# Retention attention and a GELU layer on one core: when each batch's loads are issued, and where batch 3's first scores stand

## The chip, the cores and the metric

The kernel runs on one core of one Trainium2 chip. Its time is the device time of one execution in microseconds (us). Before the change three runs took 295.61, 297.89 and 301.87 us, so the median is 297.89 us. A fourth execution was recorded by the hardware profiler; it took 295.5 us, and all views of the profile below are of that one.

## The reference, cut to what matters

```python
def _attn_ref(q, k, v):                       # (8, 8, 576, 64) each: batch, head, position, head width
    scores = scale * np.matmul(q, k.transpose(0, 1, 3, 2))
    gamma = 1.0 - 2.0 ** (-5.0 - np.arange(H))
    rel = pos[:, None] - pos[None, :]
    Dmat = np.where(rel >= 0, gamma[:, None, None] ** rel[None, :, :], 0.0)
    return np.matmul(scores * Dmat[None], v)

def _moe_ref(x, w_in, w_out):                 # x: 4608 x 512, w_in: 512 x 2048, w_out: 2048 x 512
    h = x @ w_in
    g = 0.5 * h * (1.0 + np.tanh(c * (h + 0.044715 * h * h * h)))
    return g @ w_out
```

The attention result of all 8 batches, with its heads side by side, is the x of the second function. Inputs and output are float32.

## The kernel before, in words

**Tiling.** A batch has 576 positions: four chunks of 128 and a tail of 64. The tails of two batches make one tile, called the tails of that pair. The second part works on blocks of 512 tokens: block t (0 to 7) is the four chunks of batch t, block 8 is made of the tails. The two parts overlap: while TensorE works through block t of the layers, it also computes, in between, the attention of batch t + 1, whose result is the x of the next block. The attention is causal with a decay, so each chunk needs its own scores (`score`, line 379), a mask (`masks`, line 389), the product with v (`av`, line 455), and what the chunks in front leave behind: a state (`state`, 402), carried on by `scan` (416) and `spread` (430) and multiplied with q in `past` (436). `put` (466) copies the finished chunk into `xT`, the input of the next block.

**Order written out by hand.** A block is a list of about 30 steps (lines 979 to 1041). In blocks 2 to 5, which matter here, steps 0 to 15 are `up` (474): four matmuls of 128x512 and a GELU on ScalarE for each. Steps 16 to 29 are `prod` (648), eight matmuls of 128x256 each, seven products computed in two halves. After every second pair of `up` steps (steps 3, 7, 11 and 15) `act_sums` (634) puts four additions on VectorE. Everything else is hung on a step by `at(t, u, f)`: after step u of block t, f is issued. The program fixes the order in which each engine gets its instructions; each engine then works through its own in that order, and waits where an input is not there.

**Attention in a block.** Lines 940 to 953 hang the attention of batch b = t + 1 into block t. `scores` (911) of chunks 0 and 1 stand after step s0, their `outs` (922: past, av, the next state, put) after step o0, the scores of chunks 2 and 3 after s1, their outs after o1. Normally (s0, o0, s1, o1) is (9, 15, 19, 25); in block 3 it is (11, 15, 19, 25). The tails of a pair go with the scores and outs of blocks 3, 4, 6 and 7 (`TP`, line 132). The scans follow one step after the outs (`later`, line 778).

**Loads, casts and transposes.** For a batch b from 2 on, 12 loads (q, k and v of four chunks, 256 KB each, `load`, line 91) go from SyncE's queue, SP, into one of 16 buffers. Each is cast to float16 by `cc` (771), k and q on GpSimd (POOL), v on ScalarE (for batch 3 on GpSimd too). The casts of batch b stand in block b - 2, from step 16 to 23 (line 958). Then `turn_dma` (305) issues two DMA transposes from SP, one for k and one for q, and, where tails go with the batch, `cast_tails` (245) casts their k and q on GpSimd and issues one more transpose, of the tile e into the tile ett. The scores of batch b in block b - 1 read what these transposes write (`tt`, `ett`).

**The queue of loads.** `seq` (line 130) lists all loads in order: the first batches and weights, then batch after batch, with an entry "t" for the loads of a pair's tails behind the batch b for which b - 1 is in `TP`. `pump` (141) issues entries from the list as long as one of the 16 buffers is free; `cc` gives a buffer back and calls it. An entry "h" makes it stop until `resume` (312), which each batch b hangs after step 29 of block b - 2 (batch 2: step 12 of block 1). Before the change "h" stands behind batches 2 and 3; from batch 4 on the queue is stopped by a line of its own from step 16, where the casts begin, to step 29. Since 16 buffers stand against 12 loads of a batch, the resume in block 1 issues the 12 loads of batch 4, the 6 of the first tails and the first 4 of batch 5; the resumes of blocks 2, 3 and 4 then issue the other 8 of a batch, its tails if any, and the first 4 of the batch after it (block 4's has none after it).

Lines that the prediction's steps touch, as they stand before:

```python
    for b in range(1, B):
        seq += body(b) if b > 1 else []
        if b in (NPE, NPE + 1):
            seq.append(("h",))
        if b - 1 in TP:
            seq.append(("t", TP[b - 1]))
...
        at(t0, 5 if b == NPE else ut[-1] + 1, lambda b=b: turn_dma(b, TP.get(b - 1)))
        at(t0, go, resume)
```

Of the kernel before, what the change touches and what calls it, by code (L numbers as in the profile page):

```python
# [20 lines left out]
def kernel(  # L21
# [22 lines left out]
    NPE = 2  # L44
# [74 lines left out]
    def parts(b):  # L119
        if b == NPE:  # L120
            return [(key, c) for c in range(NC) for key in "kq"] + [("v", c) for c in range(NC)]
        return [(key, c) for c in range(NC) for key in "kqv"]

    def body(b):
        if b < NPE:
            return [("b", b, key, 2 * g + y) for g in range(2) for key in "qkv" for y in range(2)]
        return [("b", b, *x) for x in parts(b)]

    QS = (0, 2, 1, 3)
    seq = body(0) + [("i", g, ct) for g in QS for ct in range(4)]  # L130
    seq += [("o", f) for f in range(NF)] + body(1)
    TP = {3: 0, 4: 2, 6: 4, 7: 6}
    for b in range(1, B):
        seq += body(b) if b > 1 else []
        if b in (NPE, NPE + 1):
            seq.append(("h",))
        if b - 1 in TP:
            seq.append(("t", TP[b - 1]))
    q_ld = {"next": 0, "free": LD, "hold": False}

    def pump(freed=0):
# [98 lines left out]
    def new_casts(b):  # L240
        a = att[b]
        for key in "kqv":
            a[key] = sb.tile([128, W], F16, tag="c" + key, name="c" + key, bufs=1 if key == "q" else 2)
# [38 lines left out]
    def new_turned(b):  # L282
        att[b]["tt"] = t = sb.tile([128, 2, NB, 128], F16, tag="tt", name="tt", bufs=2)
        att[b]["tk"], att[b]["tq"] = t[:, 0], t[:, 1]
# [20 lines left out]
    def turn_dma(b, tails=None):  # L305
        a = att[b]
        for key in "kq":
            nc.sync.dma_start_transpose(out=a["t" + key], in_=a[key])
        if tails is not None:
            cast_tails(tails)  # L310
# [460 lines left out]
    def cc(b, key, c, eng):  # L771
        cast(b, key, c, eng)
        pump(1)
# [4 lines left out]
    def later(b, c):  # L778
        scan(b, c)
        spread(b, c, A.copy)  # L780
# [53 lines left out]
    def at(t, u, f, last=False):  # L834
        events.setdefault((t, u, last), []).append(f)
# [75 lines left out]
    def scores(t, c, tails=None):  # L911
        b = t + 1
        if b < B:
            score(b, c), score(b, c + 1)
        if tails is not None:
            score(PAIR + tails, 0)
        if b < B:
            masks(b, c), masks(b, c + 1)
        if tails is not None:
            masks(PAIR + tails, 0)  # L920

    def outs(t, c, tails=None, ahead=None):
        b = t + 1
        work = [(b, c), (b, c + 1)] if b < B else []
        if tails is not None:
            work.append((PAIR + tails, 0))
        for w in work:
            past(*w)
        for w in work:
            av(*w)  # L930
        if ahead is not None:
            state(*ahead)
        for w in work:
            put(*w)

    U2 = (21, 23, 25, 28)
# [2 lines left out]
        at(1, 17 + c, lambda c=c: later(2, c))  # L939
    for t in range(1, B):  # L940
        b, tl = t + 1, TP.get(t)
        s0, o0, s1, o1 = U2 if t == 1 else (11, 15, 19, 25) if t == 3 else (9, 15, 19, 25)
        at(t, s0, lambda t=t, tl=tl: scores(t, 0, tl))
        at(t, o0, lambda t=t, b=b, tl=tl: outs(t, 0, tl, (b, 2, 3) if t < B - 1 else None))
        if b == B:
            continue
        at(t, s1, lambda t=t, b=b: scores(t, 2))
        at(t, o0 + 1, lambda b=b: later(b, 2))
        at(t, o1, lambda t=t, nb=b + 1: outs(t, 2, None, (nb, 0, 1) if nb < B else None))
        at(t, min(o1 + 1, 29), lambda b=b: later(b, 3))  # L950
        if b + 1 < B:
            for c in range(2):
                at(t + 1, c, lambda c=c, nb=b + 1: later(nb, c))

    for b in range(NPE, B):
        ent = parts(b)
        eng = {"k": P, "q": P, "v": P if b == NPE + 1 else A}
        t0, ut, go = b - 2, [16, 16, 17, 18, 18, 19, 20, 20, 21, 22, 22, 23], 29
        if b == NPE + 1:
            ut = [16, 16, 17, 19, 19, 20, 22, 22, 23, 24, 24, 25]  # L960
        if b == NPE:
            t0, ut, go = 1, [0, 0, 0, 0, 2, 2, 4, 4, 6, 7, 9, 10], 12
        at(t0, ut[0], lambda b=b: (new_casts(b), new_turned(b)))
        if b > NPE + 1:
            at(t0, ut[0], lambda: q_ld.update(hold=True))
        if b > NPE:
            at(t0, ut[0], lambda t=t0: nc.gpsimd.tensor_copy(out=gate, in_=gs[t]["4"][:, NH - 1, 1, 0:1]))  # L967
        for u, (key, c) in zip(ut, ent):
            at(t0, u, lambda b=b, key=key, c=c, e=eng[key]: cc(b, key, c, e))
        at(t0, 5 if b == NPE else ut[-1] + 1, lambda b=b: turn_dma(b, TP.get(b - 1)))  # L970
        at(t0, go, resume)
# [101 lines left out]
```

## Time and profile before

| what | value |
|---|---|
| time of the profiled execution | 295.5 us |
| its span, first to last instruction | 293.7 us |
| TensorE (PE) busy | 281.8 us, 96% |
| VectorE (DVE) busy | 201.0 us, 68% |
| ScalarE (ACT) busy | 169.5 us, 58% |
| GpSimd (POOL) busy | 99.9 us, 34% |
| granted TensorE clock | 0.995 of full |
| DMA, mean over the span | 184 GB/s |

The span and the time differ by 1.8 us that lie around the instructions. Busy time of an engine is the time in which it worked on an instruction; PE's weight loads are counted apart. "SP" is the engine that issues the DMAs; an entry of its queue in the timeline begins when it starts to issue a DMA and is as long as the issuing takes, while the data land some microseconds later. A wait is put down to what came last. Block 2 of the layers runs from 84.6 to 114.5 us, block 3 to 146.2, block 4 to 176.8, block 5 to 206.7.

### The profile page before, as it was taken

The page shows a single profiled execution, that of the slowest core. Times are in us where ns is not written, and L with a number is a line of the kernel's source. Part 1 is how long each engine was busy: PE and PEld are TensorE (multiplying, and loading weights), DVE is VectorE, ACT ScalarE, POOL GpSimd, SP SyncE. Part 2 cuts the span into 40 slices and gives each one's busy share as a digit, 9 for nine tenths or more (in the row PEclk, how much of TensorE's full clock was granted, in tenths as well). Part 3 has the DMA queues.
Part 4 walks back from the last instruction along what each step waited for, and adds up shares of the span by engine and source line. Part 5 has one row for each costly group of instructions (what it writes and reads, how often), then busy time and mean ns, then how long its engine had stood idle before and what let it go on. Part 6 is the DMA issues. An engine that isn't in the chain of part 4 may idle for free. (4 is left out here: it accounts for less than half of the span.)

```text
span 293.7 us, 7393 instructions
## 1 busy us (share of the span) xinstructions
PE 281.8 (96%) x3028; PEld 208.1 (71%) x3028; DVE 201.0 (68%) x409; ACT 169.5 (58%) x320; POOL 99.9 (34%) x129
## 2 busy tenths in 40 slices
PE   6989998999999999989999999999999999999993
PEld 3568876888864687458845884488548887887782
DVE  6796988656864873487448744765488968975863
ACT  5287754996338546855486647664665268507800
POOL 4689669901760184008500740068030000000000
PEclk9999999999999999999999999999999999999998
DMA  7999999999989999999999999995941030002013
GB/s 209 311 366 378 364 286 244 248 241 191 222 131 260 229 211 190 202 267 209 194 209 252 223 208 235 222 137 90 242 100 38 2 143 3 0 38 107 3 36 107
DMA packets 139361, 53.95 MB, mean 184 GB/s; under 512 B 118080, under 2 KB 130880, under 8 KB 139328
## 3 DMA queue, kind: packets, MB, share of 16 engines
q1 hardware_dynamic: 138848, 52.97, 80.8%
q8 instruction: 23, 0.38, 0.6%
q10 hardware_dynamic: 480, 0.52, 0.6%
q14 instruction: 10, 0.08, 0.1%
HBM read 36.70 MB, written 9.44 MB: 157 GB/s over the span
## 5 line engine op out<-in xcount | busy, mean ns | idle before, releaser
L480 PE MATMUL hp<-xT,w_in_sb 128*128 128x512 f16 x352 | 79.0, 380 | 0.0
L486 ACT ACTIVATE gT<-hp 128x512 f16<-128x512 f32 x88 | 50.1, 600 | 26.5 <-PE hp L480 26.0
L665 PEld LDWEIGHTS <-gT 128*128 128x128 f16 x576 | 54.9, 98 | 9.1 <-issue 1.3
L480 PEld LDWEIGHTS <-w_in_sb 128*128 128x128 f16 x352 | 34.1, 98 | 38.1
L665 PEld LDWEIGHTS <-s 128*128 128x128 f16 x432 | 41.7, 98 | 5.3
L642 DVE TENSOR_TENSOR s<-gT 128x512 f16<-128x512 f16 x36 | 15.6, 434 | 31.8 <-ACT gT L486 25.1
L665 PE MATMUL opA<-w_out_sb,gT 128*128 128x256 f16 x288 | 35.3, 273 | 0.7 <-ACT w_out_sb L765 0.6
L392 DVE TENSOR_TENSOR ret<-st,cm 128x512 f16<-128x512 f32 x48 | 29.7, 682 | 3.8 <-PE st L383 3.8
L501 PE MATMUL hp<-xT,w_in_sb 128*128 128x256 f16 x256 | 29.2, 273 | 0.3 <-POOL w_in_sb L765 0.3
L967 POOL COPY gate<-s 128x1 f16<-128x1 f16 x5 | 0.9, 188 | 82.6 <-DVE s L646 82.6
L434 ACT CAST tbd<-ws 64x256 f16<-64x256 f32 x48 | 19.3, 403 | 13.8 <-DVE ws L425 13.2
L501 PEld LDWEIGHTS <-w_in_sb 128*128 128x128 f16 x256 | 24.5, 98 | 3.6 <-POOL w_in_sb L765 0.6
L665 PE MATMUL opB<-wt,gT 128*128 128x256 f16 x224 | 26.8, 273 | 0.1
L275 POOL TENSOR_TENSOR ck<-ld,sc 128x512 f16<-128x512 f32 x24 | 25.0, 1040 | 4.4 <-DMA ld<-in_k_dram 4.4
L275 POOL TENSOR_TENSOR cq<-ld,sc 128x512 f16<-128x512 f32 x24 | 25.9, 1078 | 0.6 <-DMA ld<-in_q_dram 0.3
L469 ACT CAST xT<-xs 128x512 f16<-128x512 f32 x36 | 19.3, 592 | 11.7 <-PE xs L459 8.5
L679 DVE TENSOR_TENSOR k<-k,opB 128x512 f32<-128x512 f32 x17 | 11.7, 686 | 13.3 <-PE opB L665 7.4
L508 ACT ACTIVATE gT<-hp 128x512 f16<-128x512 f32 x32 | 18.4, 602 | 3.6 <-PE hp L501 3.5
L262 ACT CAST cv<-ld 128x512 f16<-128x512 f32 x23 | 13.4, 618 | 11.9 <-DMA ld<-in_v_dram 11.7
L665 PE MATMUL opB<-wt,s 128*128 128x256 f16 x144 | 17.4, 273 | 0.0
L665 PE MATMUL opC<-wt,s 128*128 128x256 f16 x144 | 17.2, 273 | 0.0
L644 DVE TENSOR_TENSOR gT<-gT 128x512 f16<-128x512 f16 x36 | 17.1, 476 | 0.0
(122 smaller groups left out, 407.1 us busy)
## 6 DMA issues: line engine op xcount, KB each, us to landing
ld<-in_q_dram SPq DMA_DIRECT2D x32, 256.0 KB, 5.2
ld<-in_k_dram SPq DMA_DIRECT2D x32, 256.0 KB, 5.2
ld<-in_v_dram SPq DMA_DIRECT2D x32, 256.0 KB, 5.4
out_dram<-ost SPq DMA_DIRECT2D x16, 512.0 KB, 3.9
ld<-in_moe_w_in_dram SPq DMA_DIRECT2D x16, 256.0 KB, 5.7
ld<-in_moe_w_out_dram SPq DMA_DIRECT2D x16, 256.0 KB, 6.0
lt<-in_k_dram SPq DMA_DIRECT2D x8, 128.0 KB, 4.6
lt<-in_q_dram SPq DMA_DIRECT2D x8, 128.0 KB, 4.4
```

The lines of the kernel that those rows point to most:

```text
L262: eng.copy(out=dst, in_=raw)
L275: eng.tensor_tensor(out=dst.rearrange("p (h d) -> p h d", d=D), in0=raw.rearrange("p (h d) -> p h d", d=D), in1=sc[:, s0].unsqueeze(2).to_ ...
L392: nc.vector.tensor_tensor(out=r.rearrange("p (n i) -> p n i", i=128), in0=t.rearrange("p (n i) -> p n i", i=128), in1=(cm if b < PAIR else ...
L434: cp(out=(tbd[b % 2][r, c, :, r] if c < NC - 1 else tbt[b % NT4][r, :, r]), in_=w[r])
L469: nc.scalar.copy(out=xT[:, g0 : g0 + 2], in_=xs.rearrange("p (n g t) -> p g n t", n=HP, g=2))
L480: nc.tensor.matmul(hp.rearrange("p (g t) -> p g t", t=TL), w_in_sb[:, ct, 128 * fc : 128 * fc + 128], xT[:, o : o + TB // TL, ct, :], star ...
L486: nc.scalar.activation(out=gT[t][:, fc].rearrange("p i n -> p (i n)"), in_=hp, func=AF.Gelu_apprx_tanh)
L501: nc.tensor.matmul(hps[n][:, 256 * x : 256 * x + 256].rearrange("p (g t) -> p g t", t=TL), w_in_sb[:, ct, 128 * (fs[n] + x) : 128 * (fs[n] ...
L508: nc.scalar.activation(out=gT[t][:, f : f + 2, 2 * u : 2 * u + 2, :].rearrange("p f i n -> p f (i n)"), in_=hp.rearrange("p (f n) -> p f n ...
L642: nc.vector.tensor_tensor(out=s["1"], in0=a21, in1=a22, op=ALU.add)
L644: nc.vector.tensor_tensor(out=a21, in0=a11, in1=a21, op=ALU.subtract)
L665: nc.tensor.matmul(op[tag][:, HD * u : HD * u + HD], lhs(f), rhs[:, f], start=(new and f == 0), stop=(f == NH - 1), skip_group_check=True,)
```

## The change

Two things. In the list of loads, an "h" now stands behind every batch from 2 to 7 (behind its tails, where it has some), and the old stop from step 16 to 29 is left for batches from 8 on, which do not exist. So each resume issues just the 12 loads of the next batch and its tails; the first 4 loads of the batch after it, which stood in front of the next transposes in SP's queue, come with the next resume. And in block 2 the scores of batch 3's chunks 0 and 1 stand after step 12 in place of 9, their outs after 16 in place of 15, with the scan that follows; the scores of chunks 2 and 3 after 20 in place of 19.

```diff
@@ -132,10 +132,10 @@
     TP = {3: 0, 4: 2, 6: 4, 7: 6}
     for b in range(1, B):
         seq += body(b) if b > 1 else []
-        if b in (NPE, NPE + 1):
-            seq.append(("h",))
         if b - 1 in TP:
             seq.append(("t", TP[b - 1]))
+        if NPE <= b < 8:
+            seq.append(("h",))
     q_ld = {"next": 0, "free": LD, "hold": False}
@@ -939,7 +939,7 @@
     for t in range(1, B):
         b, tl = t + 1, TP.get(t)
-        s0, o0, s1, o1 = U2 if t == 1 else (11, 15, 19, 25) if t == 3 else (9, 15, 19, 25)
+        s0, o0, s1, o1 = U2 if t == 1 else (12, 16, 20, 25) if t == 2 else (11, 15, 19, 25) if t == 3 else (9, 15, 19, 25)
@@ -961,7 +961,7 @@
         at(t0, ut[0], lambda b=b: (new_casts(b), new_turned(b)))
-        if b > NPE + 1:
+        if b >= 8:
             at(t0, ut[0], lambda: q_ld.update(hold=True))
```

## The prediction

> **What bounds the kernel now.** I read the busy times first, then TensorE's (PE) own waits, then the same by block, and then followed the one wait that counts back through SP's queue.
>
> The page, and the waits of PE:
>
> ```profile
> PE 281.8 (96%) x3028; PEld 208.1 (71%) x3028; DVE 201.0 (68%) x409; ACT 169.5 (58%) x320; POOL 99.9 (34%) x129
> ...
> PE st L383 <- DMA ett<-e: 0.5, 1, 0.5
> ...
> PE st L383 <- DMA tt<-cq: 0.5, 1, 0.5
> ```
>
> PE is busy for 281.8 of 293.7 us. Of the 11.9 us left, most lie in the first 50 us and the last 14, where the change does nothing. So it can bring little; the two waits above, for transposed tiles, are what it can reach. Where they are is seen by blocks 2, 3, 4 and 5 (columns: stretch, its length, busy time and instructions of PE, PEld, DVE, ACT, POOL, the granted clock, DMA share, GB/s):
>
> ```profile
> 84.59:114.47 29.88, 29.88 (x287) 20.18 (x285) 18.71 (x38) 18.18 (x36) 11.89 (x13) 1.00 1.11 209
> 114.47:146.24 31.77, 30.80 (x310) 20.92 (x308) 19.03 (x38) 18.92 (x36) 11.49 (x12) 1.00 1.06 215
> 146.24:176.80 30.56, 30.56 (x311) 20.91 (x308) 18.92 (x38) 18.83 (x36) 8.37 (x9) 1.00 1.12 219
> 176.80:206.68 29.88, 29.88 (x287) 20.19 (x285) 17.82 (x36) 17.81 (x34) 10.58 (x11) 1.00 0.97 168
> ```
>
> Blocks 3 and 4 do the same work (both with tails): 31.77 against 30.56. Block 3 loses 1.21 us; blocks 2, 4 and 5 lose nothing that PE shows. The place, in PE's timeline:
>
> ```profile
> 114.47 10.52 PE L480 MATMUL hp<-xT,w_in_sb 128*128 128x512 f16 x48
> 125.46 0.62 PE L383 MATMUL st<-tt 64*128 64x128 f16 x16 [0.47 <-DMA tt<-cq]
> 126.59 0.40 PE L383 MATMUL st<-ett 64*128 64x128 f16 x8 [0.50 <-DMA ett<-e]
> ```
>
> And what SP did before that:
>
> ```profile
> 107.72 1.61 SPq L86 DMA_DIRECT2D lt<-in_k_dram  x2
> 109.38 1.31 SPq L86 DMA_DIRECT2D lt<-in_q_dram  x2
> 110.74 1.31 SPq L86 DMA_DIRECT2D lt<-in_v_dram  x2
> 112.09 0.63 SPq L101 DMA_DIRECT2D ld<-in_k_dram  x1
> 112.77 1.93 SPq L101 DMA_DIRECT2D ld<-in_q_dram  x1
> 114.75 1.30 SPq L101 DMA_DIRECT2D ld<-in_v_dram  x1
> 116.14 1.17 SPq L101 DMA_DIRECT2D ld<-in_k_dram  x1
> 117.42 3.38 SPq L308 DMA_TRANSPOSE tt<-ck  x1
> 120.89 2.13 SPq L308 DMA_TRANSPOSE tt<-cq  x1
> 123.11 1.61 SPq L252 DMA_TRANSPOSE ett<-e  x1
> ```
>
> SP has no pause. The transposes of batch 4 stand behind the tails and behind four loads of batch 5 (112.09 to 117.42), though their inputs were ready: in POOL's timeline the last k cast ends at 110.08, the last q cast at 111.27, the second cast of e at 116.34. Landing times of these three from the issue: 5.2, 4.4 and 3.4 us, so q lands at 125.3 and e at 126.5, just where PE resumes. The neighbours are near the edge too. Batch 3's q lands at 88.42 + 4.4 = 92.8, and its scores start at 93.32. Batch 5's q lands at 149.50 + 4.9 = 154.4 (scores 154.97), its e at 151.91 + 3.4 = 155.3 (wanted at 155.43). Batches 6 and 7 have over 5 us to spare (q at 179.8 for 185.53, and at 209.8 for 215.40).
>
> **The change part by part.**
>
> *Four loads taken from in front of batch 4's transposes.* SP reaches the k transpose at 112.09, when its casts are done: 5.33 us earlier. By the durations above k takes SP to 115.5, q (cast at 111.27) to 117.7, e (cast at 116.34) to 119.3. With the landings above q is there at 119.9 and e at 121.1, against 124.99 where PE wants them. Both waits go: **-1.2 us**, the 1.21 by which block 3 exceeds block 4. Between bounds: the two waits alone are 0.97, and nothing else in block 3 waits on PE. I take 1.2. Behind it stand the masks on VectorE: four at 2.48 us together and two at 1.28, begun about 0.4 after the first score, end near 129.1; the av that reads them would come about 129.85. 0.7 us to spare, no new wait.
>
> *The same in block 3 for batch 5.* What came later at the old place comes at the new one: the two output stores go right behind e (from 124.82 to about 119.3, their sums being done at 113.6 and 115.4), and then 12 loads in place of 8. Twelve loads took 91.72 to 107.72, 16.0 us, in block 2, and 16.65 from 154.41, so 1.33 to 1.39 each. From 121.3 that is 137.3 to 138, then the tails (4.5, as from 136.89 to 141.41) to about 142. In the old order 8 loads and the tails ended at 141.41. So loads end where they did, and the k transpose goes out at 142 in place of 146.08 (the casts end near 141.3). q lands at about 150.3, e at 150.7, wanted at 153.8 (PE is 1.2 earlier): 3 us to spare in place of 0.1. PE did not wait here, so **0** in this profile.
>
> *Blocks 4 and 5.* By the same steps batch 6's 12 loads end near 166.4, its transposes wait for the casts (about 170.5, against 171.06), batch 7's loads and tails end near 199 in place of 193.4. Its transposes start at 201.18 in both cases, since they waited 8.6 us there for casts that start at 193.79. **0**; if that cover went, batch 7's spare 5 us would be used first.
>
> *Who else waits for a load.* The v loads are cast on ScalarE, in line with the copies that free banks and fill xT. The last v of batch 5 was issued at 135.53, landed at 141.0, and ScalarE had waited 3.19 us for it; behind it stand 0.62 + 0.58 + 1.07 us of cast, copy and put, with the next block's first matmul at 146.24 (145.0 when shifted). It may land at 142.7 without cost. In the new order it is the twelfth load: 121.3 + 11 x 1.33 to 1.39 = 135.9 to 136.6, landing 5.5 later at 141.4 to 142.1. Cover of 0.6 to 1.3 us, so **0**, and the thinnest place of this change. In a sentence aside: the Trainium skill, DMA: Bandwidth & Descriptors (Where 436 GB/s comes from) puts the limit of HBM for one core at about 358 GB/s, by which a load of 256 KB would take an estimated 0.73 us, twelve 8.8, and this place would have 6 us of cover; the rows here, 1.33 to 1.39, speak against it for these loads, and the forecast goes by the rows.
>
> *Batch 3's scores three steps later.* PE's order changes, not its work. In block 2 no wait is seen at 93.32, so the gain is 0 here; the spare time of 0.5 us becomes 0.5 + 3 x 0.86 = 3.1. The loss can come from the masks: they now stand behind the additions of step 11 on VectorE, which wait for a GELU near 95.9 and take 1.5; four masks of 2.48 then end near 99.9, and the last av needs them at about 100.2 (four steps of 0.86 to 0.87 after the scores). Between 0 and +0.5; I take 0, since the additions of step 15 begin at 99.89 in both orders and block 3 lives with the same four steps. The other moves by one step: scores at 20 leave 4.4 us for 2.48 of masks. 0.
>
> **Sum:** 295.5 - 1.2 = 294.3 us for the profiled execution (span 292.5). The median of the runs shown is 2.4 above the profiled one, the lowest run 0.1. The same 1.2 off the profiled one and the two lowest runs gives 294.3, 294.4 and 296.7, mean 295.1; as waits near the edge may be a part of that scatter, I forecast **295.0**.
>
> **The rivals.**
> *No gain.* The transposes start earlier but land no earlier, or e is the last one held by its cast. For it: e's cast needs the tails' loads, and POOL waited 1.96 and 1.03 us for them. Against it: the cast ended at 116.34, so e would have to land 5 us later than it does after an issue. Then the time is as before, 295.5 to 297.9, about 296.7.
> *A larger gain.* Three batches in a row have 0.5 us or less to spare, so in slower executions each delay of the DMA falls on PE, up to the 2.4 us of the median and the 6.4 of the highest run. The change gives each 3 us or more. If all the scatter is that, the runs come to 294.3 or below and a comparison with slower runs of before, near 300, passes 2%. For it only the margins speak; no profiled row shows such a wait.
> *Slower: the late v load.* The mechanism is ScalarE waiting for the twelfth load, so that xT is late and PE stands at the start of the next block. It decides when that load lands after 142.7 in block 3, 1 us later than the sum has it. Single loads took SP 3.02 and 2.46 us in the trace; two such in one batch add 2.8. Block 3 would then lose 2.8 - 1.0 = 1.8, block 4 (where ScalarE waited 1.37 us for PE behind its v, so a little more cover) 1.4: 294.3 + 3.2 = 297.5 for the profile, 298.2 beside the median's habits. To lose 6 us, loads of 1.8 us each would be needed; no stretch shows that.
>
> **How the numbers follow.** Forecast 0.62, no gain 0.14, larger gain 0.09, slower 0.15. About 2% (6 us) is what a measurement of this kernel can tell from no change; the forecast and the first rival lie within it. Of the larger gain 0.06 passes 2%, of the slower case 0.06. That makes 0.06 faster, 0.88 the same, 0.06 slower. The range goes from 293.0 (1.2 more than the sum, by the margins) to 299.0 (the slower case and a median like before's).
>
> **What would show it.** Right: the k transpose of block 2 starts near 112 with no load of batch 5 in front; no wait of PE for tt or ett at line 383; block 3 about 30.6 us long; blocks 2, 4 and 5 as before; SP with short pauses in front of transposes. Wrong: a stretch of block 2 over 29.9 with a wait for ret (the masks), a first matmul of block 4 or 5 that waits for xT behind a v cast, or the waits at ett still there.

## The result, and the profile after

The changed kernel takes 295.17 us (median of 20 runs, 293.24 to 296.52); the kernel before, in as many runs beside it, 297.67 us (295.29 to 302.39). The ratio is 0.9937, 95% interval 0.991 to 0.9965: a gain of about 0.6%, clear of noise and well within 2%. (The medians differ by 0.8%; the gain by the ratio is smaller because the ratio leaves the longest executions out, and only the kernel before had them.) The forecast was 295.0.

The profiled execution after took 293.7 us with a span of 291.9, 1.8 us less than before. Here are blocks 2, 3 and 4 by stretches, with the same columns as in the prediction:

```profile
83.58:113.89 30.31, 30.04 (x287) 20.19 (x284) 20.57 (x39) 17.36 (x35) 12.58 (x15) 1.00 1.10 214
113.89:144.44 30.55, 30.55 (x308) 20.89 (x308) 19.71 (x38) 19.37 (x38) 11.40 (x13) 1.00 1.09 216
144.44:175.00 30.56, 30.56 (x311) 20.89 (x309) 18.91 (x38) 18.83 (x36) 9.09 (x10) 1.00 1.04 210
```

Block 3 is 30.55 us in place of 31.77, and 30.56 is what block 4 takes for the same work. So the 1.8 us are made of: block 2 begins 1.01 earlier (83.58 against 84.59, in code that the change does not touch), block 2 is 0.43 longer (30.31 against 29.88), block 3 is 1.22 shorter, and from block 4 on nothing differs (116.9 us from 175.00 and from 176.80 to the end). The first of these is scatter: over the profiles of this study block 2 begins anywhere from 83.5 to 86.3 us. The second cannot be put down to the change either, as the section on the late v load shows: the same wait is there, and longer, in a run with the old queue. What belongs to the change is the 1.22 of block 3.

PE's timeline in block 3, and SP's queue ahead of it:

```profile
113.89 10.52 PE L480 MATMUL hp<-xT,w_in_sb 128*128 128x512 f16 x48 [0.27 <-ACT xT L469]
124.34 0.62 PE L383 MATMUL st<-tt 64*128 64x128 f16 x16
124.80 0.39 PE L383 MATMUL st<-ett 64*128 64x128 f16 x8
```

```profile
110.81 2.38 SPq L86 DMA_DIRECT2D lt<-in_v_dram  x2
113.30 2.97 SPq L308 DMA_TRANSPOSE tt<-ck  x1
116.37 1.35 SPq L308 DMA_TRANSPOSE tt<-cq  x1
117.81 2.02 SPq L252 DMA_TRANSPOSE ett<-e  x1
121.29 0.92 SPq L101 DMA_DIRECT2D ld<-in_k_dram  x1
```

No load stands between the tails and the k transpose; it starts at 113.30 in place of 117.42, and the scores wait for neither tt nor ett. SP now pauses, from 165.1 to 169.05, in front of batch 6's transposes, whose casts it waits for: the place where four loads stood. What the first profile did not have is the 0.27 us in the first line: the first matmul of block 3 waits for xT, which ScalarE fills. (It delays PE by 0.43 us: the 16 matmuls ahead of it are listed with 1.91 us, but where nothing waits the next one starts 1.75 us after them.)

### The profile page after: what moved, and what is told of

The parts are those of the page before. It is cut to its first block, busy times and chain, and to the rows that moved or that the text cites. A ratio compares the mean times of both kernels' runs of the same rounds, so it can differ in the third digit from the quotient of the medians.

```text
span 291.9 us, 7394 instructions
## 1 busy us (share of the span) xinstructions
PE 281.6 (96%) x3028; PEld 208.1 (71%) x3028; DVE 203.9 (70%) x409; ACT 169.2 (58%) x320; POOL 100.5 (34%) x129
## 5 line engine op out<-in xcount | busy, mean ns | idle before, releaser
L425 DVE TENSOR_TENSOR ws<-vs,gt 128x256 f32<-128x256 f32 x24 | 16.8, 702 | 1.2
```

The source lines that it names most:

```text
L425: nc.vector.tensor_tensor(out=w, in0=uc, in1=gt, op=ALU.mult)
```

## The experiments

**Theory Q**: the gain comes from transposes that stood behind four loads in SP's queue and landed when PE already wanted them. **Theory S**, its rival: the moved steps of block 2 are what pays, since batch 3's q landed 0.5 us ahead of its scores. Later came **theory V** (a late v load is what the changed kernel still loses) and **theory C** (a wait of PE costs more than its length).

### One part of the change at a time

The queue of loads alone, with block 2's steps as before:

```diff
-        s0, o0, s1, o1 = U2 if t == 1 else (12, 16, 20, 25) if t == 2 else (11, 15, 19, 25) if t == 3 else (9, 15, 19, 25)
+        s0, o0, s1, o1 = U2 if t == 1 else (11, 15, 19, 25) if t == 3 else (9, 15, 19, 25)
```

> The change's queue of loads alone: each batch's loads held until the transposes of the batch in front are issued; batch 3's scores back after step 9 of block 2. Theory Q (the transposes of batches 4 and 5 stood too late in SP's queue): block 3 is 30.6 us as after the change, no wait for ett, and the ratio to before is 0.994 to 0.997, so at least half of the whole change's 0.9937; batch 3's scores at step 9 keep their 0.5 us of spare time and the executions scatter a little more than the changed kernel's. Theory S (the scores' place in block 2 is what pays, since batch 3's q lands 0.5 us before it is wanted): ratio 0.998 to 1.002, with block 3 still cured by 1.2 us but the executions as scattered as before (7 us between lowest and highest).

Measured: ratio 0.9937 (0.9906 to 0.9967), 295.26 us median of 12 runs (294.40 to 297.49). That is the whole change's ratio. Block 3 takes 30.56 us, and its scores follow without a wait:

```profile
125.44 0.62 PE L383 MATMUL st<-tt 64*128 64x128 f16 x16
125.90 0.39 PE L383 MATMUL st<-ett 64*128 64x128 f16 x8
```

The moved steps alone, with the queue as before (the diff's second hunk without the others):

> The moved steps of block 2 alone, with the queue of loads as before. Theory Q: block 3 keeps its waits for tt and ett (about 1 us together, block 3 at 31.5 us or more), ratio 0.997 to 1.001. Theory S: ratio 0.994 or below, scatter as small as the changed kernel's (3.3 us). Both: block 2 itself stays at 29.9 to 30.2 us.

Measured: ratio 1.0005 (0.9976 to 1.0035), 297.60 us median (295.84 to 301.66), scatter as wide as before. Theory S falls: the moved steps bring nothing that can be measured, in the median or in the spread. The profile caught an execution of 298.14 us, and it showed what I had not counted. Block 2 is 30.85 us, not the 29.9 to 30.2 that were written down: block 3 begins with a wait of 0.81 us for xT, with the loads queued as before. PE's timeline and then stretches of it (length, busy times, granted clock third from the end):

```profile
114.37 10.52 PE L480 MATMUL hp<-xT,w_in_sb 128*128 128x512 f16 x48 [0.81 <-ACT xT L469]
126.19 0.62 PE L383 MATMUL st<-tt 64*128 64x128 f16 x16 [1.30 <-DMA tt<-cq]
127.23 0.40 PE L383 MATMUL st<-ett 64*128 64x128 f16 x8 [0.42 <-DMA ett<-e]
127.56 5.31 PE L480 MATMUL hp<-xT,w_in_sb 128*128 128x512 f16 x16
```

```profile
127.56:129.20 1.64, 1.64 (x10) 0.64 (x7) 1.64 (x4) 0.21 (x1) 0.00 (x0) 0.67 1.02 334
129.20:131.20 2.00, 2.00 (x6) 0.73 (x5) 1.97 (x5) 0.89 (x2) 0.00 (x0) 0.50 1.08 218
131.20:132.70 1.50, 1.50 (x7) 0.64 (x6) 0.54 (x2) 0.69 (x2) 0.00 (x0) 0.89 1.37 233
```

The 16 matmuls behind the waits take 5.31 us in place of 3.63, at a granted clock of 0.67, 0.50 and 0.89. The clock lost in the three stretches is 0.54 + 1.00 + 0.17 = 1.7 us, as much as 3.4 us at half clock. Block 3 is 34.21 us long: 1.72 of waits and 1.68 of lowered clock over the 30.55 without either, and 0.26 besides (in the first profile waits of 0.97 came with 1.21, so 0.24 besides). A row of busy time hides this, since the slow matmuls count as busy: PE's share in block 3 is 32.49 us there and 30.80 in the first profile.

### Moving the reader in place of the writer

The queue as before; the scores of blocks 3 and 4 moved back too:

```diff
-        s0, o0, s1, o1 = U2 if t == 1 else (11, 15, 19, 25) if t == 3 else (9, 15, 19, 25)
+        s0, o0, s1, o1 = U2 if t == 1 else (12, 16, 20, 25) if t in (2, 4) else (14, 18, 21, 25) if t == 3 else (9, 15, 19, 25)
```

> Queue of loads as before, but the scores that read late transposes are moved back instead: block 2 at steps 12, 16, 20, 25 as in the change, block 3 at 14, 18, 21, 25 (before 11, 15, 19, 25), block 4 at 12, 16, 20, 25 (before 9, 15, 19, 25). 3 steps are 2.6 us, more than the 1.0 us by which batch 4's transposes come too late. Theory Q in its wide form (all that counts is that the transposed tiles are there when PE wants them, whichever of the two is moved): no wait for tt or ett, block 3 at 30.6 to 30.9 us, ratio 0.993 to 0.996 as the change itself. If the load order matters by itself (less traffic around the transposes, or v loads that come at another time): ratio 0.997 to 1.000 though the waits for tt and ett are gone.

Measured: ratio 0.9927 (0.9895 to 0.9958), 295.59 us median of 12 runs (294.21 to 297.35). The waits for tt and ett are gone and the time is the changed kernel's, with the old order of loads. So theory Q holds in its wide form: it counts that the tile is there when its reader comes, and the order of the loads has no worth of its own that can be measured. One expectation missed: block 3 is 31.48 us in place of 30.6 to 30.9, since the masks now stand ahead of the last additions on VectorE, and a product waits for those (the ratio does not resolve these 0.9 us):

```profile
134.18 0.39 PE L665 MATMUL opB<-wt,s 128*128 128x256 f16 x2 [0.74 <-DVE s L643]
```

### Two loads ahead in place of four or none

```diff
-        seq += body(b) if b > 1 else []
+        seq += body(b)[2 if b > NPE + 1 else 0 :] if b > 1 else []
...
+        if NPE < b < B - 1:
+            seq += body(b + 1)[:2]
         if NPE <= b < 8:
             seq.append(("h",))
```

> The changed kernel, but two loads of the batch after next are again issued in front of the transposes (before: four, changed: none), for batches 4 to 6. Two loads took SP 2.7 us, so batch 4's q lands at about 122.5 and its e near 123.8, against 124.3 where PE wants them in the changed kernel: 0.5 us to spare. Theory Q: no wait in a fast profile, block 3 30.6 us, and the ratio lies between, 0.994 to 0.998, with more scatter than the changed kernel. Theory S: as the changed kernel, 0.9937.

Measured: ratio 0.9894 (0.9856 to 0.9932), 294.45 us median of 6 runs. Block 3 is 30.55 us and does not wait (batch 3's q, which now has two loads of batch 4 in front of it, holds its scores for 0.18 us in block 2). The ratio was lower than theory Q had it, so it was run again beside the changed kernel:

> Two loads ahead once more, because its first ratio, 0.9894 (0.9856 to 0.9932) from 6 runs, was below what theory Q gave (0.994 to 0.998). If that was chance: 0.992 to 0.996, the median within 0.5 us of the changed kernel's in this call. If two loads ahead are truly better than none (SP has no pause in front of the transposes, and the loads behind them come earlier): the median 0.5 us or more below the changed kernel's.

> The changed kernel again, on the chip of this call, so that the others can be held against it: ratio 0.991 to 0.9965, median near 295.2. The profile may be of an execution other than the first one; its waits of PE in blocks 2 to 5 say what the changed kernel still loses: by theory V it is the first matmul of block 3 waiting for xT, and no wait for tt or ett.

Measured beside each other: two loads ahead 0.9902 (0.9869 to 0.9934), 294.90 us; the changed kernel 0.9903 (0.9871 to 0.9935), 294.77 us. They cannot be told apart. Both lie below what was written down, 0.992 to 0.996 and 0.991 to 0.9965, and the changed kernel's own ratio differs by 0.3% between the two times it was measured (0.9937 and 0.9903), so the low 0.9894 does not speak for two loads ahead. They leave enough room: what pays is to be off the edge, and more room brings nothing that can be measured.

### What is left: the late v load

In the changed kernel's second profile block 2 is 30.63 us long, and again the first matmul of block 3 waits for xT, 0.59 us. ScalarE's timeline there (idle time before, and its cause, in brackets):

```profile
113.12 0.62 ACT L262 CAST cv<-ld 128x512 f16<-128x512 f32 x1 [3.43 <-DMA ld<-in_v_dram]
113.65 0.58 ACT L729 COPY ost<-opA 128x512 f32<-128x512 f32 x1
114.12 1.07 ACT L469 CAST xT<-xs 128x512 f16<-128x512 f32 x2
```

ScalarE stands 3.43 us before the last v chunk of batch 4; then come the copy and the put, which ends at 115.19, just where PE starts block 3 (115.25).

This wait does not come from the change. In the nine profiles in which batch 4's twelve loads are issued in one row and ScalarE casts the last v, xT is ready 21.6 to 22.2 us after the first of these loads, in either order of the queue, while block 2 alone takes 29.87 us. So PE has to wait where the loads begin later than some 7.9 us after the start of block 2. They began 8.29 and 8.69 us after that start in the changed kernel's two profiles and 8.88 in the run with the steps alone, which has the old queue; those three have the wait, 0.27, 0.59 and 0.81 us. The six others, three of the kernel before and the loads alone among them, began at 6.90 to 7.94 us and do not have it. The moved steps have no part in when the loads begin: SP goes without a pause from batch 3's k transpose to them, and that transpose goes out 0.5 to 2.7 us after the block's start, well ahead of the first moved step.

To take the wait away, the last v cast of batches 4 to 7 goes to GpSimd:

```diff
-            at(t0, u, lambda b=b, key=key, c=c, e=eng[key]: cc(b, key, c, e))
+            e = P if key == "v" and c == 3 and b > NPE + 1 else eng[key]
+            at(t0, u, lambda b=b, key=key, c=c, e=e: cc(b, key, c, e))
```

> The changed kernel with the cast of the last v chunk of batches 4 to 7 moved from ScalarE to GpSimd. Theory V (what is left in the changed kernel's block 2 is ScalarE waiting 3 us for batch 4's twelfth load, so that xT is late and the first matmul of block 3 waits, 0.27 us in its profile and more in others): no wait of PE for xT at the start of block 3, ratio to before 0.988 to 0.992, 0.5 to 1.5 us below the changed kernel in the same call. Rival (the wait is too small, or GpSimd's extra 0.6 us puts the tails' casts and e's transpose back): ratio 0.992 to 0.996, the same as the changed kernel.

> Two loads of the next batch ahead of the transposes, as in the run with two loads ahead, and the last v cast of batches 4 to 7 on GpSimd. Theory V: both together, ratio 0.986 to 0.990, scatter under 2.5 us. Rival: as two loads ahead alone (0.9894), since that one already keeps SP busier.

Measured: 0.9902 (0.9867 to 0.9938), 294.83 us on the changed kernel; 0.9905 (0.9868 to 0.9942), 294.67 us with two loads ahead as well. In the first one's profile the wait for xT is gone and block 2 is 29.87 us, though the loads begin 8.31 us after its start: the mechanism is as theory V has it. Its size is not: 294.83 against 294.77 for the changed kernel beside it, where 0.5 to 1.5 us less was written down, and 0.9905 where it was 0.986 to 0.990. What these few executions (6 to 8 of each, within 2 to 3 us) do not exclude is a gain as small as the listed waits, 0.3 to 0.6 us.

### The price of a wait, and other executions of the kernel before

One and a half more loads in front of batch 4's transposes alone, in the kernel before:

```diff
+        if b == 4:
+            for n, t in enumerate(junk):
+                nc.sync.dma_start(
+                    out=t.rearrange("p (h d) -> p h d", d=D),
+                    in_=q[n, 0 : H >> n, 0:128, :].rearrange("h s d -> s h d"),
+                )
         for key in "kq":
             nc.sync.dma_start_transpose(out=a["t" + key], in_=a[key])
```

> The kernel before, with one and a half more loads (256 and 128 KB that nobody reads) put in front of batch 4's transposes, so that these go out about 2 us later still: the suspected cost is made larger in one place. A wait of its own size (theory W): block 3 grows from 31.8 to about 33.8 us and the time by 2 us, ratio 1.007. A wait that also lowers the granted clock (theory C, from the run with the steps alone, where gaps of 1.3 and 0.4 us were followed by a clock of 0.5 for some 3 us): block 3 is 35 us or more, the clock falls under 0.9 between 127 and 134 us, ratio 1.010 to 1.016. If theory Q is wrong and the loads in front do not delay the transposes: block 3 at 31.8 and ratio 1.0.

Measured: ratio 1.0081 (1.0047 to 1.0116), 299.37 us median of 10 runs against 297.27. PE's timeline and the stretches behind the wait:

```profile
127.40 0.62 PE L391 MATMUL st<-tt 64*128 64x128 f16 x16 [2.68 <-DMA tt<-cq]
128.52 0.40 PE L391 MATMUL st<-ett 64*128 64x128 f16 x8 [0.50 <-DMA ett<-e]
128.85 5.31 PE L488 MATMUL hp<-xT,w_in_sb 128*128 128x512 f16 x16
```

```profile
128.85:130.50 1.65, 1.65 (x9) 0.62 (x6) 1.65 (x4) 0.00 (x0) 0.00 (x0) 0.54 1.02 330
130.50:132.50 2.00, 2.00 (x7) 0.71 (x6) 1.97 (x5) 0.70 (x2) 0.00 (x0) 0.53 1.09 221
132.50:134.00 1.50, 1.50 (x8) 0.68 (x7) 0.46 (x2) 1.09 (x2) 0.00 (x0) 1.00 1.37 227
```

SP spends 2.72 us on the added loads, the wait for tt grows from 0.47 to 2.68, and the clock falls behind it as in the run with the steps alone (0.76 + 0.94 = 1.7 us lost). Block 3 is 35.67 us, 3.9 more than the first profile's 31.77: 2.2 of wait and 1.7 of clock. In the trace theory C holds and a wait of its own size does not (33.8). The ratio alone lies between the two figures that were written down, 1.007 and 1.010, and its interval holds both; it can't decide.

Then the kernel before was profiled twice more, since its first profile was among its fastest executions:

> The kernel before, profiled once more, since its first profile (295.5 us) is one of its fastest executions, 2 us under the median. Theory Q with C: an execution near the median (297.5) has longer waits for tt and ett in block 3, or in blocks 2 and 4 too, with or without a lowered clock after them, and blocks 5 on as before. Rival: the extra time lies in the first 84 us, where the profiles so far differ by 2.8 us and which the change does not reach.

> The same once more: a third profile of the kernel before, with the same two expectations, because a single execution says little about scatter. Theory Q with C: blocks 2 to 4 together are 93 us or more (92.2 in the first profile, 91.4 in the changed kernel). Rival: they are 92.2 or less and the first 84 us are longer.

Measured: 296.08 and 296.27 us. Blocks 2, 3 and 4 of the first of them, and the wait in block 4:

```profile
84.12:114.06 29.94, 29.94 (x287) 20.24 (x284) 19.82 (x38) 17.56 (x35) 12.82 (x15) 1.00 1.09 217
114.06:146.19 32.13, 30.80 (x310) 20.96 (x308) 19.65 (x38) 19.56 (x38) 11.56 (x13) 1.00 1.02 214
146.19:177.45 31.26, 30.73 (x310) 20.92 (x308) 18.93 (x38) 18.83 (x36) 8.37 (x9) 1.00 1.12 221
```

```profile
156.07 0.40 PE L383 MATMUL st<-ett 64*128 64x128 f16 x8 [0.53 <-DMA ett<-e]
```

The other has 29.87, 31.91 and 31.37 and waits 0.64 us at the same place. So batch 5's e, which the first profile had 0.1 us ahead of its reader, comes too late in both of these; block 4 loses 0.7 and 0.8 us. Blocks 2 to 4 together take 93.3 and 93.2 us, against 92.2 in the first profile, and 91.4, 91.7 and 91.0 in three profiles with the new queue (the changed kernel twice, the loads alone). The new profiles begin block 2 at 84.1 and 84.6 us, no later than the first: the rival, that the extra time lies in the first 84 us, does not hold for them. But at 296.1 and 296.3 us neither is an execution near the median of 297.3, which the first expectation was about; no profile of the kernel before is.

## Why the prediction was right

**The wait removed: right.** The sum took 1.2 us off block 3; it lost 1.22. The rows bore out the rest of that step: the k transpose starts at 113.30 (112.09 in the prediction; the tails' v loads took SP 2.38 us in place of 1.31), e lands at 117.81 + 4.2 = 122.0 (121.1), PE wants it at 124.80.

**Where the stall could go: right in kind, wrong in place.** Batch 5's loads and tails end at 142.0 as forecast, its k transpose starts at 142.15, q and e land at 149.6 and 150.6. Twelve loads took SP 15.6 us (121.29 to 136.88), 1.30 each. The estimate of 0.73 us by the Trainium skill, DMA: Bandwidth & Descriptors (Where 436 GB/s comes from), is not what these loads show, and the rows were the right choice. (The cover worked out beside it is about 8 us by that estimate, 142.7 - 121.3 - 11 x 0.73 - 5.5, and not 6; nothing hangs on it.) The v load was named as the thinnest place, and so it was, but for batch 4 in block 2, whose loads the change does not move, and not for batch 5 in block 3, where the last v is cast at 140.59 in time. The prediction gave block 2 nothing and looked there for late masks. The masks ended at 98.88, ahead of their reader; the 0.43 us came through xT. The prediction read no wait there from one execution, in which the loads began 7.13 us into the block; where they begin later the wait is there, in the old queue too.

**"PE did not wait here, so 0 in this profile": mis-sized for the median.** The step on batch 5 read a margin of 0.1 us in one fast execution as no cost. The two other profiles of before show 0.7 to 0.8 us there. The price of a wait was taken as its length as well, while a gap of 1.3 and 0.4 us cost another 1.7 in lowered clock. Both bear on the rival of a larger gain: its mechanism, margins so thin that executions scatter over them, is shown by block 4 in the two profiles, and the median fell by 2.5 us, more than the 1.2 of the sum. How much of the 2.5 these waits are is not shown. It stayed within 2%. That 295.0 met 295.17 owes something to the choice of averaging the lowest runs with the profile, which stood in for what the sum lacked. The profiled execution itself came to 293.7 against the sum's 294.3; the 0.6 us between are the earlier start of block 2 less its longer end, and so scatter.

**The moved steps: 0 was right.** The 3.1 us of room that they give batch 3 are not needed: in none of the profiles with its scores at step 9 is PE listed as waiting for its q, though in one of them q lands at 92.8 for scores at 92.91. With two loads ahead the room is used: there PE waits 0.18 us in one profile in spite of it.

**What stays open**: how much of the gain is clock that no longer falls. The three profiles of the kernel before do not have the fall; the run with the steps alone, with the same queue, does. The mean granted clock of whole executions, where it is on record, says a little more: it is below 0.995 in 8 of 55 executions of the kernel before, in 3 of 12 with the steps alone and in 7 of 10 with the added loads, and in none of the 76 of the changed kernel and of the runs that take the waits away. Where in those executions it fell is not on record.

## What to carry to other kernels

When an engine waits for a transfer, look at what stands in front of it in its queue: prefetches that are not yet needed can hold up a transfer whose reader is near, and either may be moved, the loads or the reader. A margin of a few tenths of a microsecond in one profile is a wait in another execution, so list the margins too and not only the waits. Enough room is enough: two loads ahead were as good as none, and taking away the next wait in line brought nothing that could be measured. And before a new wait is put down to a change, look for it in the runs without the change.

## What the runs showed of the hardware that was not expected

Gaps of 1.3 and 2.7 us, each with a shorter one behind it, were enough here to lower TensorE's granted clock. With 1.30 and 0.42 us idle around 0.6 us of small matmuls, the clock went to 0.50 for about 3.4 us, by the three stretches, at a price of 1.7 us; after 2.68 and 0.50 us the price was the same 1.7; with 0.84 and 0.50 us the clock stayed at 1.00. Where between these the limit lies was not measured. The Trainium skill, TensorE: Matmul & The Clock Gate (Why this matters for your kernels), asks for no idle gaps over about 3 us; here gaps of less than half of that were enough, in a stretch of 2.7 us with little work, so the measurement decides.
